# Q/K and first FFN contract in paired 64-row halves: seven steps of two halves that swap banks, in place of three full tiles and a 64-row rest

## The chip, the cores and the metric

The kernel runs on one core of one Trainium2 chip. The metric is the device time of one execution in microseconds (us); lower is better. TensorE is called PE, VectorE DVE, ScalarE ACT, GpSimd POOL and the DMA-issuing SyncE SP, as in the profile; PEld is PE's weight load.

## The reference

One adaLN transformer block with a sliding local dilated attention and a SiLU FFN, in bf16, batch 1, 2048 tokens, model width 448, 16 heads of 28, FFN width 1792:

```python
mod = (_silu(c) @ w_mod).reshape(c.shape[0], 6, 1, -1)
sa, ca, ga, sb, cb, gb = (mod[:, i] for i in range(6))   # shifts, scales, gates
h = _layernorm(x) * (1 + ca) + sa
x = x + ga * attention(h, wqkv, wo)      # 8 keys: positions s, s-2, ..., s-14
h = _layernorm(x) * (1 + cb) + sb
x = x + gb * (_silu(h @ w1) @ w2)
```

Each token attends to eight keys of its own parity (dilation 2, window 8). The contract dimension of Q, K, V, of the output projection and of the first FFN product is 448, which is three and a half times the 128 rows of PE's array; that of the second FFN product is 1792, fourteen times 128.

## The kernel before, in words

Tokens come in four chunks of 512 (NC = 4); within a chunk, even and odd positions are kept apart (`par`, 256 each). Every chunk goes through layer norm 1, the projections to Q, K and V, the attention in blocks of 112 or 128 queries (nine blocks by two parities), the output projection, layer norm 2, and two FFN products.

**The contract of 448.** Normalised activations are transposed so that the 448 features lie on partitions in four tiles that start at features 0, 128, 192 and 320 (`ROW`), so that tiles 1 and 2 overlap by 64. `tile_of(k, way)` gives for a "way" 0 or 1 three full tiles (0, 1 + way, 3) and as a fourth the 64 rows that are left: way 0 finds them in the upper 64 partitions of tile 2, way 1 in the lower 64 of tile 1. Two products, one of each way, thus have three 128-row matmuls each and one 64-row matmul in opposite halves of the array. These two run side by side. Weights for the rest rows are kept apart (`wp3` for Q and K, `w13` for the FFN).

**`duo`** (L556) writes this for Q and K (L619, 128 weights by 512 tokens, group pairs g, g+1) and for the first FFN product (L790, hidden tiles i and i + 7). A "member" of a duo is one double PSUM bank `[128, 2, 512]`, in which bank j holds the way-j product. A pair of members has two steps on PE, which may be separated by other work: `first` runs the six full matmuls of member 0, its two rest halves, and the two rest halves of member 1; `second` runs the six full matmuls of member 1. Member 0 is read out after `first`, member 1 after `second`. There are 8 pairs of Q/K, 12 pairs in the first FFN product, and 4 lone members there (i = 6) that have six full matmuls and two halves.

**PSUM.** Three double banks (`big`) serve V, Q/K, the logits (two at a time), the output projection and the first FFN product; two single banks (`one`) serve the attention's values and the second FFN product. A double bank is reused only when its reader is done: ACT or DVE casts (`qk<-ps_qk`, L623), ACT's exponentials (`p<-ps_l`, L679), ACT's SiLU (`both<-ps_h`, L794; it writes the tile named `both`, the hidden activations).

**Row modes.** PE works on 128 rows (most matmuls), on 64 (the rest halves of L619, L643, L763 and L790) or on 28 rows of a quarter (the logits, L671). V and the output projection place their rest halves first or last, by the parity of the block.

**The order.** The program is built as a list of operations with dependencies; `ORDER` is a list written out by hand that fixes the order in which they are issued, and by it the order on each engine. Each engine takes its instructions in that order. SP issues all DMAs, among them the transposes of normalised activations (`h<-xn`) and of attention outputs (`oT<-o`). The change leaves `ORDER` and the number of operations as they are.

A second copy of the whole layer (`safe`) stands behind a branch that is taken when a softmax sum is out of range; it isn't run here.

Of the kernel before, what the change touches and what calls it, by code (L numbers as in the profile page):

```python
# [16 lines left out]
H = 16  # L17
# [15 lines left out]
CP = 256  # L33
# [41 lines left out]
def half(j):  # L75
    return slice(K3 * j, K3 * j + K3)
# [8 lines left out]
def tile_of(k, way):  # L85

    return (slice(0, 128), (0, 1 + way, 3)[k]) if k < 3 else (half(1 - way), 2 - way)
# [129 lines left out]
def layer(ctx, tc, io, safe):  # L217
# [5 lines left out]
    V, S, G, T = nc.vector, nc.scalar, nc.gpsimd, nc.tensor  # L223
# [10 lines left out]
    def ct(shape, name, dt=BF16):  # L234
        return const.tile(shape, dt, name=name)

    def bigt(name):
        return big.tile([128, 2, 512], F32, name=name, tag="big")
# [17 lines left out]
    wp = ct([128, 3, 2 * H, 32], "wp")  # L256
    wp3 = ct([128, H, 32], "wp3")
# [3 lines left out]
    w1 = ct([128, 3, F], "w1")  # L261
    w13 = ct([128, F // 2], "w13")
# [41 lines left out]
    def none(o):  # L304
        pass

    P = Plan()
    for r, n in (("big", 3), ("one", 2), ("v", NV), ("p", NP), ("xn", NX), ("o0", 2), ("o1", 2), ("out", len(outb))):
        P.resource(r, n)

    def copy_on(o):
        return S.copy if o["eng"] == "act" else V.tensor_copy

    def either(act, dve):
        return [("act", act), ("dve", dve)]

    def act_ns(n):
        return 55.0 + 0.833 * n

    def dve_ns(n):  # L320
        return 75.0 + 1.04 * n

    P.resource("dma", 8)
    begin = P.op(("sp", 1630.0), none)

    def sp(ns, fn, deps, land=0.0, give=()):

        a = P.op(("sp", ns), fn, deps, take=("dma",))  # L330
        return P.op(("none", land), none, [a], give=((a, "dma"),) + tuple(give)), a

# [5 lines left out]
    def first_x(i):  # L338
        return dict(out=x_all[:, 2 * i:2 * i + 2, :].rearrange("p t d -> p (t d)"), in_=x_view[0, :, i, :])
    act_q = [P.op(("none", 0.0), lambda o: nc.scalar.dma_start(**first_x(1)))]  # L340
    act_q.append(P.op(("none", 0.0), lambda o: nc.scalar.dma_start(out=c4[0:3, :], in_=c[:, 0:384].rearrange("o (k p) -> (o k) p", p=128)), act_q[-1:]))
# [214 lines left out]
    def duo(mms, name, n, deps, evacs, table=None):  # L556


        held = {}
        ns = n / 2.4 + 2.0  # L560

        def first(o):
            p0 = held[0] = bigt(name)
            for j in range(2):
                for k in range(3):
                    mms[0](p0, j, k, k == 0, False)
            if len(mms) > 1:
                held[1] = bigt(name)
            for j in range(2):
                mms[0](p0, j, 3, False, True)  # L570
            if len(mms) > 1:
                for j in range(2):
                    mms[1](held[1], j, 3, True, False)

        def second(o):
            for j in range(2):
                for k in range(3):
                    mms[1](held[1], j, k, False, k == 2)
        mm = [P.op(("pe", 6 * ns + 110.0 + len(mms) * (ns + 12.0)), first, deps, take=("big",) * len(mms), mac=(6 + len(mms)) * ns, mode=(0, 1))]
        if len(mms) > 1:  # L580
            mm.append(P.op(("pe", 6 * ns + 5.0), second, [mm[0]], mac=6 * ns))
        out_ = []
        for i, ev in enumerate(evacs):
            last = [P.op(on, lambda o, f=f, i=i: f(o, held[i]), [mm[i]] + d, table=table) for on, f, d in ev]
            P.op(("none", 0.0), none, last, give=((mm[0], "big"),))
            out_.append(last)
        return mm, out_
# [23 lines left out]
    def project(k):  # L611
        h = h1[k % NH]
        s0 = CP * k

        def mm(g):
            def f(ps, j, kk, start, stop):
                rows, t = tile_of(kk, j)
                w = wp[:, kk, H * j + 4 * g:H * j + 4 * g + 4, :] if kk < 3 else wp3[rows, 4 * g:4 * g + 4, :]
                T.matmul(ps[:, j, :], lhsT=w.rearrange("p h d -> p (h d)"), rhs=h[rows, :, t, 128:128 + CP], start=start, stop=stop)  # L619
            return f  # L620

        def ev(g):
            return [(either(act_ns(1024), dve_ns(1024)), lambda o, ps: copy_on(o)(out=qk[:, :, g, :, s0:s0 + CP], in_=ps[:].rearrange("p j (t s) -> p j t s", t=2)), [])]  # L623
        qk_done[k], qk_mm[k], v_mm[k] = [], [], []
        for g in (0, 2):
            m, ev_ = duo([mm(g), mm(g + 1)], "ps_qk", 512, h1_done[k] + pads, [ev(g), ev(g + 1)])
            qk_mm[k] += m
            qk_done[k] += ev_[0] + ev_[1]

        def vev(o, ps, b):  # L630
            v_of[b] = vb[o["slot"]["v"]]
            copy_on(o)(out=v_of[b][:, :, :, 0:DH], in_=ps[:, :, 0:D].rearrange("p j (h d) -> p j h d", d=DH))
        for b in BLOCKS[k]:
            held = {}

            def vmm(o, b=b, held=held):
                ps = held[0] = bigt("ps_v")
                b0 = 128 + 112 * b - CP * k
                ks = (0, 1, 2, 3) if b % 2 == 0 else (3, 0, 1, 2)
                for kk in ks:  # L640
                    for par in range(2):
                        rows, t = tile_of(kk, par)
                        T.matmul(ps[:, par, 0:D], lhsT=h[rows, par, t, b0:b0 + 128], rhs=wv[rows, t, :], start=(kk == ks[0]), stop=(kk == ks[-1]))  # L643
            a = P.op(("pe", 1440.0), vmm, h1_done[k] + ([halo[k]] if k else []) + ld_v, take=("big",), mac=1309.0, mode=(b % 2, 1 - b % 2))
            v_mm[k].append(a)
            v_op[b] = a
            v_take[b] = P.op(either(act_ns(2 * D), dve_ns(2 * D)), lambda o, b=b, held=held: vev(o, held[0], b), [a] + v_ready, take=("v",), give=((a, "big"),))
# [129 lines left out]
    def us_of(k):  # L777
        return [4 * k + j for j in range(4)]

    def ffn1(k, after, l_before):  # L780
        h = h2[k % 2]
        nrm = Norm(us_of(k), x1_done, after=f1_read.get(k - 2, []), how=HOW2[k], scratch=screp[:].rearrange("p k n -> p (k n)")[:, 0:D])
        nrm.on_dma(lambda j: h[:, j:j + 2, :, :].rearrange("p j k t -> p (j k) t"), lambda t: h[:, :, t, :], 2, [mod2])

        def mm(i):
            def f(ps, j, kk, start, stop):
                rows, t = tile_of(kk, j)
                c0 = 128 * (i + 7 * j)
                w = w1[:, kk, c0:c0 + 128] if kk < 3 else w13[rows, 128 * i:128 * i + 128]
                T.matmul(ps[:, j, :], lhsT=w, rhs=h[rows, :, t, :], start=start, stop=stop)  # L790
            return f

        def ev(i):
            return [(("act", act_ns(1024)), lambda o, ps: S.activation(out=hid[:, k % 2, :, i, :], in_=ps[:], func=ACTF.Silu), after + f2_read.get(k - 2, []) + wmod_read)]  # L794
        f1_read[k], silus[k] = [], []
        for i in (0, 2, 4, 6):
            ii = [i, i + 1] if i < 6 else [i]
            mm_, ev_ = duo([mm(x) for x in ii], "ps_h", 512, nrm.done + ld_1 + l_before, [ev(x) for x in ii], table="s")
            f1_read[k] += mm_
            for e in ev_:  # L800
                silus[k] += e
# [93 lines left out]
@with_exitstack  # L895
def kernel(
    ctx: ExitStack,
    tc: tile.TileContext,
    A_x: bass.AP,
    A_wqkv: bass.AP,  # L900
    A_wo: bass.AP,
    B_x: bass.AP,
    B_w1: bass.AP,
    B_w2: bass.AP,
    c: bass.AP,
    w_mod: bass.AP,
    out: bass.AP,
):
    io = (A_x, A_wqkv, A_wo, B_w1, B_w2, c, w_mod, out)
    with ExitStack() as first:  # L910
        with tc.manual_schedule():
            bad = layer(first, tc, io, False)
    with tc.If(bad > 0, label="safe"):
        with ExitStack() as again:
            layer(again, tc, io, True)
# [30 lines left out]
```

## Time and profile before

| | us |
|---|---|
| median of 3 runs | 182.13 (181.04 to 182.39) |
| the profiled execution | 181.66 |
| its span, first to last instruction | 179.6 |
| mean granted TensorE clock | 0.994 of full speed |
| L790 (first FFN product), PE busy | 47.3, 224 matmuls |
| L812 (second FFN product), PE busy | 46.1, 224 matmuls |
| L619 (Q and K), PE busy | 26.8, 128 matmuls (20.0 and 6.8 in two groups, by the names of their tiles) |
| L794 (SiLU on ACT), busy | 28.0, 28 activations |

A row of the page's list of groups gives line, engine, operation, what is written from what, shapes and count; then busy time, the mean of one in ns, and the idle time of the engine just before such an instruction with what ended it. Matmuls are pipelined: a matmul of 512 columns is shown with 380 ns, but the next one starts 216 ns after it, so that the starts, not the durations, tell what a step costs. The chain that ended last is given as start, length, engine, tile, line and count; on a busy PE, a length there is the distance between the first starts of two groups.

### The profile page before, as it was taken

How to read it: one execution, taken by the hardware profiler on the slowest of the kernel's cores; microseconds unless marked ns; L12 is line 12 of the kernel's file. 1: busy time of each engine (PE TensorE's matmuls, PEld its weight loads, DVE VectorE, ACT ScalarE, POOL GpSimd, SP SyncE). 2: the span in 40 equal slices, each digit the busy share in tenths (PEclk: the TensorE clock that was granted, in tenths of full speed). 3: DMA queues.
4: the chain of work that ended last, by engine and by line, in shares of the span. 5: the costliest groups of instructions: out<-in, count | busy, mean ns of one | idle time of the engine just before them, and what ended most of it. 6: DMA issues, size and time to landing. Idle time of an engine off the chain costs nothing.

```text
span 179.6 us, 3554 instructions
## 1 busy us (share of the span) xinstructions
PE 168.7 (94%) x1406; PEld 76.7 (43%) x1406; DVE 103.9 (58%) x219; ACT 110.1 (61%) x153; POOL 26.1 (15%) x86
## 2 busy tenths in 40 slices
PE   7999999888889999999999999999999998999990
PEld 2543333444345344344544445554434444434540
DVE  5699797699798988364378135984633311200211
ACT  2277939897779657779999649643596322244200
POOL 4656540000012220022000000023040000000000
PEclk9999999999999999999999999999999999999997
DMA  5993569956682223102400013125307000010021
GB/s 199 333 344 89 143 143 305 336 117 152 185 251 55 51 62 84 26 0 62 58 26 4 26 26 80 29 55 135 84 0 194 5 0 26 0 51 4 29 79 35
DMA packets 33343, 17.42 MB, mean 97 GB/s; under 512 B 24296, under 2 KB 32936, under 8 KB 33320
## 3 DMA queue, kind: packets, MB, share of 16 engines
q1 hardware_dynamic: 33168, 16.90, 35.0%
q8 instruction: 13, 0.21, 0.5%
q10 hardware_dynamic: 152, 0.23, 0.4%
q14 instruction: 10, 0.08, 0.2%
HBM read 9.12 MB, written 1.84 MB: 61 GB/s over the span
## 4 chain that ended last, share of the span: by engine, by line
PE 70%; DVE 10%; DMA 7%; ACT 6%; POOL 3%; issue 2%; SPq 0%; ACTq 0%; DVEq 0%
PE ps_h L790 25%; PE ps_y L812 24%; PE ps_wo L763 7%; PE ps_qk L619 5%; PE ps_v L643 4%; ACT p L679 2%; PE ps_o L729 2%; DMA oT<-o 2%; DMA x_all<-in_A_x_dram 2%; DVE p L703 2%; DVE st L455 2%; PE ps_l L671 2%; ACT xn L483 2%; DMA wqk<-xn 2%; DMA h<-xn 2%
## 5 line engine op out<-in xcount | busy, mean ns | idle before, releaser
L790 PE MATMUL ps_h<-h,w 128*128 128x512 bf16 (+1 forms) x224 | 47.3, 380 | 0.0
L812 PE MATMUL ps_y<-w,both 128*128 128x448 bf16 x224 | 46.1, 353 | 0.6 <-DVE flag L884 0.6
L794 ACT ACTIVATE both<-ps_h 128x1024 bf16<-128x1024 f32 x28 | 28.0, 1022 | 26.0 <-PE ps_h L790 25.9
L679 ACT ACTIVATE p<-ps_l 128x896 bf16<-128x896 f32 (+1 forms) x36 | 30.7, 933 | 2.2 <-PE ps_l L671 2.1
L812 PEld LDWEIGHTS <-both 128*128 128x128 bf16 x224 | 20.8, 98 | 20.6 <-issue 1.6
L790 PEld LDWEIGHTS <-w 128*128 128x128 bf16 (+1 forms) x224 | 16.9, 96 | 27.0 <-issue 11.4
L817 DVE TENSOR_TENSOR ot<-ps_y,x_all 128x448 bf16<-128x448 f32 x16 | 9.8, 621 | 30.2 <-PE ps_y L812 30.1
L619 PE MATMUL ps_qk<-h,wp 128*128 128x512 bf16 (+1 forms) x96 | 20.0, 380 | 0.4 <-DVE h L542 0.4
L703 DVE TENSOR_TENSOR p<-p,maskb 128x1792 bf16<-128x1792 bf16 (+1 forms) x18 | 19.5, 1098 | 0.5 <-ACT p L679 0.5
L465 ACT ACTIVATE screp<-x_all,mv 128x448 bf16<-128x448 bf16 x16 | 10.7, 666 | 9.9 <-POOL mv L462 9.5
L619 PEld LDWEIGHTS <-wp 128*128 128x128 bf16 (+1 forms) x128 | 9.3, 97 | 16.1 <-issue 6.1
L462 POOL TENSOR_SCALAR mv<-sums 128x2 f32<-128x2 f32 x10 | 3.4, 343 | 76.0 <-DVE x_all L766 75.9
L766 DVE SCALAR_TENSOR_TENSOR x_all<-ps_wo,x_all 128x448 bf16<-128x448 f32 x16 | 9.5, 620 | 7.7 <-PE ps_wo L763 7.7
L485 DVE TENSOR_SCALAR xn<-x_all,mv,rs 128x512 bf16<-128x512 bf16 x23 | 8.8, 406 | 8.6 <-POOL rs L472 8.4
L763 PE MATMUL ps_wo<-wo,oT 128*128 128x448 bf16 (+1 forms) x64 | 12.5, 354 | 1.0 <-DMA oT<-o 0.6
L643 PE MATMUL ps_v<-wv,h 128*128 128x448 bf16 (+1 forms) x56 | 11.1, 354 | 1.0 <-ACT p L679 0.7
L623 DVE CAST qk<-ps_qk 128x1024 bf16<-128x1024 f32 x10 | 12.0, 1214 | 0.1
L472 POOL TENSOR_TENSOR rs<-rs,negh 128x2 f32<-128x2 f32 x16 | 11.5, 717 | 1.3
L735 DVE TENSOR_TENSOR o<-ps_o,rc 112x448 bf16<-112x448 f32 (+1 forms) x18 | 11.2, 624 | 0.6
L729 PE MATMUL ps_o<-v,p 128*128 128x29 bf16 x288 | 9.6, 176 | 1.2 <-DVE gbc L438 0.6
L542 DVE TENSOR_SCALAR h<-h,modc 128x512 bf16<-128x512 bf16 x15 | 5.6, 407 | 8.6 <-DMA h<-xn 8.6
L729 PEld LDWEIGHTS <-p 128*128 128x128 bf16 x288 | 8.8, 96 | 4.1 <-DVE p L703 0.9
(85 smaller groups left out, 147.9 us busy)
## 6 DMA issues: line engine op xcount, KB each, us to landing
out_dram<-ot SPq DMA_DIRECT2D x16, 112.0 KB, 1.7
both<-in_w_mod_dram SPq DMA_DIRECT2D x2, 672.0 KB, 5.7
x_all<-in_A_x_dram SPq DMA_DIRECT2D x3, 448.0 KB, 5.8
w<-in_B_w_dram SPq DMA_DIRECT2D x3, 448.0 KB, 6.0
w<-in_B_w_dram SPq DMA_DIRECT2D x1, 896.0 KB, 5.0
both<-in_w_mod_dram SPq DMA_DIRECT2D x2, 336.0 KB, 3.4
w<-in_B_w_dram SPq DMA_DIRECT2D x1, 672.0 KB, 5.2
wv<-in_A_wqkv_dram SPq DMA_DIRECT2D x2, 224.0 KB, 5.0
```

Source lines behind the costliest of these rows:

```text
L472: G.tensor_tensor(out=rs[:, j:j + n], in0=rs[:, j:j + n], in1=negh[:, 0:n], op=ALU.pow)
L619: T.matmul(ps[:, j, :], lhsT=w.rearrange("p h d -> p (h d)"), rhs=h[rows, :, t, 128:128 + CP], start=start, stop=stop)
L623: return [(either(act_ns(1024), dve_ns(1024)), lambda o, ps: copy_on(o)(out=qk[:, :, g, :, s0:s0 + CP], in_=ps[:].rearrange("p j (t s) -> ...
L643: T.matmul(ps[:, par, 0:D], lhsT=h[rows, par, t, b0:b0 + 128], rhs=wv[rows, t, :], start=(kk == ks[0]), stop=(kk == ks[-1]))
L679: S.activation(out=out_, in_=ps[:, :, 0:4 * nq].rearrange("p j (g q) -> p j g q", q=nq), func=ACTF.Exp, scale=SCALE)
L703: V.tensor_tensor(out=p, in0=p, in1=maskb[:, 1 if b == 0 else 0, 0:nq].unsqueeze(1).to_broadcast([128, H, nq]), op=ALU.mult)
L729: T.matmul(ps[:, h, 0:DH + 1], lhsT=p[:, at:at + 128], rhs=v[:, h, 0:DH + 1], start=True, stop=True)
L735: V.tensor_tensor(out=box["o"][0:nq, off:off + D].rearrange("p (h d) -> p h d", d=DH), in0=ps[0:nq, :, 0:DH], in1=r.unsqueeze(2).to_broadc ...
L763: T.matmul(ps[:, par, 0:D], lhsT=oT[rows, kk, par, s0:s0 + 128], rhs=wo[rows, par, kk, :], start=(q == qs[0]), stop=(q == qs[-1]))
L790: T.matmul(ps[:, j, :], lhsT=w, rhs=h[rows, :, t, :], start=start, stop=stop)
L794: return [(("act", act_ns(1024)), lambda o, ps: S.activation(out=hid[:, k % 2, :, i, :], in_=ps[:], func=ACTF.Silu), after + f2_read.get(k ...
L812: T.matmul(box["ps"][:, 0:D], lhsT=hid[:, k % 2, f % 2, f // 2, 128 * j:128 * j + 128], rhs=w2[:, f // 2 + 7 * (f % 2), :], start=(f == 0) ...
```

## The change

Only `duo` and the two functions that give it its matmuls (`mm` in `project` and in `ffn1`) change, and only for pairs in the main copy; the lone members and the `safe` copy keep the old order.

Every matmul of a pair now has 64 rows. A full 128-row tile is issued as two matmuls, `part` 0 on partitions 0 to 63 and `part` 1 on 64 to 127. In the **straight** part of a member, four steps, the lower half goes to bank 1 and the upper half to bank 0 (the rest rows kk = 3 lie that way by themselves: bank j uses half 1 - j). In the **crossed** part, three steps, the lower half goes to bank 0 and the upper to bank 1. Two matmuls of one step thus lie in opposite halves of the array and write different banks. After a straight part comes a drain marked fusable that increments a semaphore `turn`; a crossed part starts with a wait for that count.

For a pair, `first` now issues straight(0), straight(1) and crossed(0): eleven steps; `second` issues crossed(1): three. Before it was eight and six. Both members' banks are taken in `first` as before, member 1's from the fifth step on.

```diff
+    turns = []
+    if not safe:
+        turn = tc.alloc_semaphore("turn")
...
     def duo(mms, name, n, deps, evacs, table=None):
...
+        def passed(i):
+            T.drain(fusable=True).then_inc(turn, 1)
+            turns.append(i)
+            wait[i] = len(turns)
+
+        def straight(i):
+            held[i] = bigt(name)
+            for kk in (0, 3, 1, 2):
+                for part in range(2):
+                    mms[i](held[i], 1 - part, kk, kk == 0, False, part)
+            passed(i)
+
+        def crossed(i):
+            T.wait_ge(turn, wait[i])
+            for kk in range(3):
+                for part in range(2):
+                    mms[i](held[i], part, kk, False, kk == 2, part)
+
         def first(o):
+            if len(mms) > 1 and not safe:
+                straight(0)
+                straight(1)
+                crossed(0)
+                return
             p0 = held[0] = bigt(name)
...
         def second(o):
+            if not safe:
+                return crossed(1)
             for j in range(2):
...
         def mm(i):
-            def f(ps, j, kk, start, stop):
+            def f(ps, j, kk, start, stop, part=None):
                 rows, t = tile_of(kk, j)
+                rows = half(part) if kk < 3 and part is not None else rows
                 c0 = 128 * (i + 7 * j)
-                w = w1[:, kk, c0:c0 + 128] if kk < 3 else w13[rows, 128 * i:128 * i + 128]
-                T.matmul(ps[:, j, :], lhsT=w, rhs=h[rows, :, t, :], start=start, stop=stop)
+                w = w1[rows, kk, c0:c0 + 128] if kk < 3 else w13[rows, 128 * i:128 * i + 128]
+                return T.matmul(ps[:, j, :], lhsT=w, rhs=h[rows, :, t, :], start=start, stop=stop)
             return f
```

`mm` of `project` changes in the same way with `wp` and `wp3`.

More of the change, by code (lines that the diff above doesn't have):

```diff
@@ L556, in duo @@
     def duo(mms, name, n, deps, evacs, table=None):
-        held = {}
+        held, wait = {}, {}
         ns = n / 2.4 + 2.0
-        def first(o):
+        def passed(i):
[13 more added lines that the diff above has]
+                    mms[i](held[i], part, kk, False, kk == 2, part)
+        def first(o):
+            if len(mms) > 1 and not safe:
[3 more added lines that the diff above has]
+                return
             p0 = held[0] = bigt(name)
@@ L615, in mm @@
         def mm(g):
-            def f(ps, j, kk, start, stop):
+            def f(ps, j, kk, start, stop, part=None):
                 rows, t = tile_of(kk, j)
-                w = wp[:, kk, H * j + 4 * g:H * j + 4 * g + 4, :] if kk < 3 else wp3[rows, 4 * g:4 * g + 4, :]
-                T.matmul(ps[:, j, :], lhsT=w.rearrange("p h d -> p (h d)"), rhs=h[rows, :, t, 128:128 + CP], start=start, stop=stop)
+                rows = half(part) if kk < 3 and part is not None else rows
+                w = wp[rows, kk, H * j + 4 * g:H * j + 4 * g + 4, :] if kk < 3 else wp3[rows, 4 * g:4 * g + 4, :]
+                return T.matmul(ps[:, j, :], lhsT=w.rearrange("p h d -> p (h d)"), rhs=h[rows, :, t, 128:128 + CP], start=start, stop=stop)
             return f
@@ L785, in mm, with f @@
         def mm(i):
-            def f(ps, j, kk, start, stop):
+            def f(ps, j, kk, start, stop, part=None):
                 rows, t = tile_of(kk, j)
+                rows = half(part) if kk < 3 and part is not None else rows
                 c0 = 128 * (i + 7 * j)
-                w = w1[:, kk, c0:c0 + 128] if kk < 3 else w13[rows, 128 * i:128 * i + 128]
-                T.matmul(ps[:, j, :], lhsT=w, rhs=h[rows, :, t, :], start=start, stop=stop)
+                w = w1[rows, kk, c0:c0 + 128] if kk < 3 else w13[rows, 128 * i:128 * i + 128]
+                return T.matmul(ps[:, j, :], lhsT=w, rhs=h[rows, :, t, :], start=start, stop=stop)
             return f
```

## The prediction

> **What bounds the kernel now.** I read the page's busy shares and its chain first:
>
> ```profile
> PE 168.7 (94%) x1406; PEld 76.7 (43%) x1406; DVE 103.9 (58%) x219; ACT 110.1 (61%) x153; POOL 26.1 (15%) x86
> PE 70%; DVE 10%; DMA 7%; ACT 6%; POOL 3%; issue 2%; SPq 0%; ACTq 0%; DVEq 0%
> ```
>
> PE (TensorE) is 70% of the chain. Where is it the bound? The table of stretches (length, then busy time by engine) says from 58.8 us on:
>
> ```profile
> 46.40:58.80 12.40, 11.24 (x168) 6.07 (x169) 10.66 (x20) 10.27 (x16) 1.62 (x4) 1.00 0.62 168
> 58.80:94.80 36.00, 35.91 (x295) 15.64 (x295) 22.89 (x44) 27.90 (x40) 4.75 (x12) 1.00 0.22 46
> 94.80:129.40 34.60, 34.60 (x326) 16.76 (x323) 21.44 (x48) 21.54 (x30) 3.04 (x10) 1.00 0.23 57
> 129.40:175.00 45.60, 44.95 (x229) 19.55 (x227) 9.46 (x22) 17.99 (x23) 2.17 (x6) 1.00 0.13 38
> ```
>
> After 58.8 PE is idle for 0.74 us in 116; what it saves or loses there is the kernel's. Before, DMA, ACT (ScalarE) and DVE (VectorE) end most waits. What a matmul step costs is in the chain in order of time (start, us, what, count):
>
> ```profile
> 77.06 6.47 PE ps_h L790 x32
> ...
> 102.66 1.30 PE ps_h L790 x6
> ...
> 104.36 3.24 PE ps_h L790 x16
> ```
>
> Six full matmuls (a pair's second half alone) take 1.30: **0.217 us a step**. A whole pair (x16) is 12 full matmuls and 2 steps in which two 64-row halves run side by side: 14 steps, 3.03, and 0.21 is left. Two pairs in a row (x32) are 28 steps, 6.07, and leave 0.40. In the starts of single matmuls the rest sits at the two changes of row mode: the step into 64 rows is 0.311, the one back 0.309, and the first after each is longer by 0.006 to 0.010. So **a change of mode costs 0.10 us**, and a pair has two.
>
> **The arithmetic of the change.** Per tile of a pair it replaces 3 full steps per bank (6) and one shared rest step by 7 steps of two halves: 7 steps either way. Twenty pairs (8 of Q/K, 12 of the first FFN contract; its four lone tiles stay) have 280 steps before and after. Matmuls go from 16 to 28 a pair, 240 more in all, and as many weight loads.
>
> *Price of a half step when many follow each other.* The trace has at most three in a row, where Q/K meets V, both in 64-row mode:
>
> ```profile
> 60.42 2.00 PE L619 MATMUL ps_qk<-h,wp 128*128 128x512 bf16 x10
> 62.25 1.59 PE L643 MATMUL ps_v<-wv,h 64*128 64x448 bf16 x8
> ```
>
> From 60.42 to 62.25 are 8 steps (1.73) and one change (0.10): nothing is left over, so two half steps and the crossing into the next group's half step cost what full ones do. The logits (L671) put four 28-row matmuls side by side for four rounds and, at 51.45 in the PE timeline, take 0.31 with their exit: 4 x 0.047 (112 columns at the full rate) and 0.10, although 8 instructions go into each 0.05 us; a half step has 4 in 0.217. Bounds: 0.213 (the crossing step just shown) and 0.226 (a first step after a change, were every step like it). I take 0.217. Over the 196 steps of the 14 pairs after 58.8 the bounds are -0.7 and +1.8 us.
>
> *The weight loads.* Of their groups, L790's has 96 ns a load; in full steps one starts 2 ns after the running matmul and ends inside its step. The trace shows two 64-row loads starting 3 ns apart under two running halves (78.30). So they are hidden at 0; were that cover gone, a step would grow by 0.096.
>
> The Trainium skill ("TensorE: Matmul & The Clock Gate", The mechanism, in Part 3) says that weight loads overlap running matmuls only where their row groups differ. The full steps, where load and matmul share all rows, contradict it; by it the price would be the last one.
>
> *Changes of mode.* I walked PE's groups in order of time and counted where the row mode changes: **104 before, 91 after**. A pair between full-row work has two either way. Pairs next to each other, or next to V, the projection or a lone tile that ends in halves, lose some (from 15.3, 25.5, 48.1, 76.9, 131.2 us). A second part that full-row work separates from its first has none now and gets two (102.5, 150.2, 163.6). Before 46.4 us 8 of 29 go, from 46.4 to 58.8 3 of 14, after that 2 of 61: 77 to 94 loses two, 129 to 148 two, 148 to 175 gains two. Worth after 58.8: 2 x 0.10 = **-0.20**.
>
> *The drains.* Two a pair, 40. They are marked fusable: the increment may ride on the matmul before them, and nothing else signals from that matmul (the results are read only after the crossed steps). Matmuls that signal today keep their 0.216 step. I take 0. If a drain stands in PE's stream and waits until the array is empty, the next load starts only then: ACT sees a tile's end 0.43 after the start of its last matmul (78.29 to 78.72), plus 0.05 for a semaphore instruction on PE's sequencer, less the step of 0.217: 0.27 each. That is the upper end.
>
> The Trainium skill ("PSUM — Partial Sum Buffer", Engine vs sequencer instructions) says that a drain waits for the engine to go fully idle; no mid-stream drain is in this trace. By it the second rival would come about.
>
> *The added waits* (`turn`). Behind them queue the crossed steps and all later PE work. The first crossed part waits for a straight part that ended four steps (0.87) earlier; the second, if it follows at once, for one whose last matmul started 0.87 earlier and signals after 0.43: 0.44 in hand, half a step's loads need 0.1. Cost 0; with nothing in hand 0.1 a pair.
>
> *What comes later.* The first tile's last step moves from the pair's 7th to its 11th: +0.57 (no change at entry, and an earlier start) to +0.87 us. Its reader and the PSUM bank it frees (three double banks) move with it. The second tile also takes its bank at step 5 instead of 8. I followed each bank and reader through the trace:
>
> - Before 46 us: readers slip by up to 0.9, but the wait on the output transposes at 46.57 (0.57 long) and the exponentials' table load at 30.2 end last. 0.
> - 46 to 59, a chain of ACT and PE:
>
> ```profile
> 49.95 1.01 ACT L623 CAST qk<-ps_qk 128x1024 bf16<-128x1024 f32 x1 [1.51 <-PE ps_qk L619]
> 51.32 0.67 ACT L465 ACTIVATE screp<-x_all,mv 128x448 bf16<-128x448 bf16 x1 [0.36 <-POOL mv L462]
> 51.98 3.32 ACT L679 ACTIVATE p<-ps_l 128x896 bf16<-128x896 f32 x4
> ...
> 53.74 1.61 PE L643 MATMUL ps_v<-wv,wqk 64*128 64x448 bf16 x8 [0.43 <-ACT p L679]
> ...
> 58.89 0.74 PE L763 MATMUL ps_wo<-wo,oT 64*128 64x448 bf16 x3 [0.44 <-ACT p L679]
> ```
>
> The pair at 48.11 starts at 48.01 (its entry change is gone), its first tile's last step at 48.01 + 10 x 0.217 = 50.18, and ACT's cast at 50.60 instead of 49.95. It ends at 51.61; L465 behind it starts there instead of at 51.32, and the exponentials, back to back with it, move by **+0.29**. PE waits for just these at 53.74 and 58.89 (last two rows), so all after them moves by 0.29. PE's three saved changes are lost in those waits.
> - 77 to 115: the pairs at 76.9 give 0.20. From 109.97 six exponentials run back to back on ACT, and two of the logits groups there start 0.04 and 0.12 after the bank they need came free. The activation before them waits behind a tile that is 0.87 later, so ACT is not earlier; I let the 0.20 be eaten: +0.20.
> - After 115: each silu that slips is read at least 0.9 us later, or runs after its pair's second tile (143.2, 152.6). 0.
>
> **Sum** on the profiled execution (181.66 us, span 179.6, so 2.06 around it): -0.20 + 0.29 + 0.20 = **+0.3, 181.95**. The median of the runs, 182.13, is 0.47 above that execution: **182.4**. A measurement of this kernel tells about 1% (1.8 us) from nothing.
>
> **Rivals.**
>
> - *Nothing is late, the saved changes stay.* The 0.29 and 0.20 vanish and the five changes from 46.4 on count: 181.6; with the eight before them too 180.8, and with half steps at the lower bound 180.1. Against it: ACT ends the waits at 53.74 and 58.89. Chance 0.08, half of it for the last two.
> - *The drains stand* (the slower side): after 58.8 28 x 0.27 = 7.6 us, and up to 12 x 0.27 = 3.2 before: **190 to 193**. It decides as soon as the increment cannot ride on the last straight matmul. For it: PE has drains today only at its start and end; against it: the marking, and one signal per matmul leaves room. Chance 0.10.
> - *Long half steps*: every one costs 0.226, so 182.4 + 1.8 = **184.2**, to 184.8 with a late `turn` here and there. For it: the only half steps next to a change are that long. Against it: the third step at 62.25. Chance 0.10.
> - *Weight loads uncovered* in half mode: 196 x 0.096 = 18.8: **201**. Against it: the loads at 78.30. Chance 0.03.
> - *It doesn't do what it says*: the halves run one after the other because they share a bank. The straight part sends them to two banks, and the signal orders the swap; I count this into the last case.
>
> **Numbers.** Forecast 182.4, chance 0.69, own range 181.6 to 183.4 (both terms of the lateness gone or doubled). 80%: **181.0 to 184.8**, which leaves out the standing drains (0.10), the uncovered loads (0.03) and half of the first rival (0.04). Faster by over 1% (under 180.3) 0.04, that half; slower by over 1% (above 183.95) 0.10 + 0.03 + 0.08 of the long steps + 0.02 = 0.23; within 1% 0.73.
>
> **What will show it.** PE 1646 matmuls; L790 in a pair alone still 3.2 us on the chain, two pairs at 77 us 6.27 instead of 6.47; no drain inside PE's stream; the weight loads' waits on issue fewer by about 13 in all; ACT's cast near 50.6; the wait at 53.74 longer. Half steps of 0.222 and more, drains with a gap of 0.27 behind them, or loads outside the matmuls would prove me wrong; so would waits of PE on silu results (L794), which I put at none.

## The result, and the profile after

The changed kernel takes **183.06 us** (median of 20 runs, 182.32 to 185.0), the kernel before 182.06 (20 runs): a ratio of **1.007, interval 1.0046 to 1.0093**. The forecast was 182.4 with 181.0 to 184.8: the sign and the range held, but the loss is 1.0 us, not 0.3, and the traces show that it comes from something that no term of the prediction named. That sign and range held all the same is luck.

The half steps themselves do what was expected. (Lines move down in the changed kernel: Q/K L619 is L651, the first FFN product L790 is L823, the cast L623 is L655, the output projection L763 is L795, the logits L671 are L703.) Chain in order of time of the changed kernel (start, us, what, count), from 104 to 109 us and from 66 to 78 us:

```profile
104.16 0.75 PE ps_h L823 x6
...
105.41 3.13 PE ps_h L823 x28
```

```profile
66.35 4.48 DMA h<-xn
70.83 0.02 issue
70.85 0.02 ACTq L544
70.86 0.05 issue
70.91 0.82 ACT h L544
71.73 0.04 issue
71.78 5.13 PE ps_h L823 x36
76.90 1.43 PE ps_wo L795 x8
```

A pair alone (x28) takes 3.13 us, 14 steps of 0.216 and one mode change, where before it was 3.24. (That is no gain: its other change of mode now falls at the end of the group ahead of it, which takes 0.50 instead of 0.39.) No drain stands in TensorE's (PE's) stream, and 1645 of the 1646 matmuls are recorded. But ahead of the first FFN contract stands a row that the chain of before does not have: the second transpose of normalised activations takes 4.48 us, and PE waits for it. The chain of before in the same place has PE alone, one group behind the other:

```profile
70.20 0.50 PE ps_o L729 x16
70.70 4.93 PE ps_h L790 x24
75.63 1.43 PE ps_wo L763 x8
```

The waits of PE (what waited, for what: us in total, times, longest), of before and then of after:

```profile
PE ps_wo L763 <- DMA oT<-o: 0.6, 1, 0.6
```

```profile
PE ps_h L823 <- ACT h L544: 1.4, 1, 1.4
...
PE ps_l L703 <- DVE qk L655: 0.7, 2, 0.5
PE ps_l L703 <- ACT qk L655: 0.6, 2, 0.3
```

One wait on a DMA has gone, and a larger one has come: PE waits for ACT's h, and ACT for the late transpose. By the starts of PE's groups in the two traces, the 1.27 us between the spans (179.55 and 180.82) are made of:

| stretch | before | after | difference |
|---|---|---|---|
| start to the output projection near 46 us | 46.57 | 46.05 | -0.52 |
| from there to the next one, near 59 us | 12.32 | 12.52 | +0.20 |
| from there to the first FFN contract | 11.66 | 13.21 | **+1.55** |
| from there to the last matmul | 104.04 | 104.01 | -0.03 |
| last matmul to the end | 4.96 | 5.03 | +0.07 |

**What delays the transpose?** The page's DMA queues name a queue that carries code:

```profile
q8 instruction: 13, 0.21, 0.5%
```

```profile
q8 instruction: 15, 0.25, 0.6%
```

The first is before, the second after (packets, MB, share of the DMA engines' time). The packets are of 16 KB and take about 1 us; between two of them PE executes some 250 instructions (matmuls and weight loads; 194 to 291 between 35 and 138 us in the two traces), so this is taken to be PE's program, loaded in blocks as PE goes along. The count of packets, and their shifts when PE's warm-up is edited below, agree with that. The change adds 240 matmuls and 240 weight loads, two blocks, and moves all the others. Before, a block came at 64.08, into the *first* transpose of that pair (4.25 us, and nothing on PE waited for it), and another at 44.5, into an oT<-o transpose that the projection at 46.57 waited for (issued at 42.65, 3.88 us). After, a block comes at 68.44, 2.09 us behind the issue of the *second* h<-xn, and none is near 44.

The Trainium skill ("Runtime: NRT & Kernel Launch", Instruction fetch mechanics) says that an engine's code is refilled in 16 KiB blocks of 256 instructions and that this is mostly hidden. The traces agree on the block (245,760 bytes in 15 packets). PE is not seen waiting for its code; what the experiments below test is whether a transpose is.

### The profile page after: what moved, and what is told of

The parts are those of the page before. It is cut to its first block, busy times and chain, and to the rows that moved or that the text cites. A ratio compares the mean times of both kernels' runs of the same rounds, so it can differ in the third digit from the quotient of the medians.

```text
span 180.8 us, 4033 instructions
## 1 busy us (share of the span) xinstructions
PE 167.9 (93%) x1645; PEld 79.3 (44%) x1646; DVE 104.1 (58%) x219; ACT 109.5 (61%) x153; POOL 25.9 (14%) x86
## 4 chain that ended last, share of the span: by engine, by line
PE 69%; DVE 9%; ACT 7%; DMA 4%; POOL 4%; issue 3%; ACTq 0%
PE ps_h L823 25%; PE ps_y L845 24%; PE ps_qk L651 7%; PE ps_wo L795 5%; PE ps_v L675 4%; DMA h<-xn 2%; PE ps_o L761 2%; ACT qk L655 2%; POOL rs L476 2%; PE ps_l L703 2%; DVE st L459 2%; DMA x_all<-in_A_x_dram 2%; ACT p L711 1%; ACT screp L469 1%; DVE p L735 1%
## 5 line engine op out<-in xcount | busy, mean ns | idle before, releaser
L823 PE MATMUL ps_h<-h,w 64*128 64x512 bf16 (+1 forms) x368 | 45.4, 377 | 1.4 <-ACT h L544 1.4
L827 ACT ACTIVATE both<-ps_h 128x1024 bf16<-128x1024 f32 x28 | 27.3, 1021 | 26.8 <-PE ps_h L823 26.7
L845 PEld LDWEIGHTS <-both 128*128 128x128 bf16 x224 | 20.3, 98 | 21.7 <-issue 4.2
L823 PEld LDWEIGHTS <-w 64*128 64x128 bf16 (+1 forms) x368 | 18.0, 94 | 26.3 <-issue 6.9
L651 PE MATMUL ps_qk<-h,wp 64*128 64x512 bf16 x168 | 19.4, 377 | 0.5 <-ACT qk L655 0.4
L651 PEld LDWEIGHTS <-wp 64*128 64x128 bf16 x224 | 11.1, 94 | 13.7 <-issue 1.5
L795 PE MATMUL ps_wo<-wo,oT 128*128 128x448 bf16 (+1 forms) x64 | 12.5, 354 | 0.4 <-ACT p L711 0.4
L655 DVE CAST qk<-ps_qk 128x1024 bf16<-128x1024 f32 x10 | 12.1, 1219 | 1.1 <-PE ps_qk L651 1.0
```

Source lines behind the costliest of these rows:

```text
L651: return T.matmul(ps[:, j, :], lhsT=w.rearrange("p h d -> p (h d)"), rhs=h[rows, :, t, 128:128 + CP], start=start, stop=stop)
L795: T.matmul(ps[:, par, 0:D], lhsT=oT[rows, kk, par, s0:s0 + 128], rhs=wo[rows, par, kk, :], start=(q == qs[0]), stop=(q == qs[-1]))
L823: return T.matmul(ps[:, j, :], lhsT=w, rhs=h[rows, :, t, :], start=start, stop=stop)
L845: T.matmul(box["ps"][:, 0:D], lhsT=hid[:, k % 2, f % 2, f // 2, 128 * j:128 * j + 128], rhs=w2[:, f // 2 + 7 * (f % 2), :], start=(f == 0) ...
```

## Experiments

**Theory 1**: a block of PE's code that is loaded while a DMA transpose is under way delays that transpose; the change moved a block into the transpose that the first FFN contract waits for, and that is the loss. **Theory 2**: the half steps, or the later end of each pair's first tile, make h late in some other way. To move the blocks without touching the work, the warm-up is edited: 27 matmuls of 512 columns at the start, whose results nobody reads. Leaving some out, or cutting some in narrower pieces, shifts every later instruction of PE against the block borders.

### The same edit in both kernels: fewer fillers

```diff
-junks = [P.op(("pe", 428.0), lambda o: warm_up(2), [w_last], mac=426.0) for _ in range(JUNK)]
+junks = [P.op(("pe", 428.0), lambda o, i=i: warm_up(2 if i < 2 else 0), [w_last], mac=426.0) for i in range(JUNK)]
```

(`i < 6` in b_j6.) The changed kernel, a_j2:

> The changed kernel with 16 of its 20 filler matmuls on TensorE left out (they only warm the engine; nothing reads them). TensorE's instructions come 32 earlier in its stream, so by the instruction positions of the changed kernel's trace the block of TensorE's code that was loaded at 68.4 us is loaded near 70.0, behind the second h<-xn transpose. Theory 1 (a code load inside a transpose's window delays its landing): that transpose takes 2.7 to 2.9 us instead of 4.48, TensorE's wait on h of 1.4 us in the first FFN contract goes, and the time is 181.5 to 182.3 us (the upper end if the block that moves from 39.4 to near 41.3 delays an oT<-o transpose there). Theory 2 (the transpose is late for another reason that the change brings, its half steps or the order of its tiles): 4.3 to 4.6 again, 182.8 to 183.4 us.

The kernel before, b_j2 and b_j6:

> The kernel before with the same 16 filler matmuls left out. Its code block of 64.1 us then comes near 67.3, into the second h<-xn transpose, and the one of 44.5 near 48.1, out of the oT<-o transposes that TensorE waits for at 46.57. Theory 1: the second h<-xn takes 4.2 to 4.6 us instead of 2.72, TensorE waits 1.2 to 1.4 us for it, and the wait of 0.57 at 46.57 goes: 182.8 to 183.5 us, the loss that the change showed, with no half step in the program. Theory 2: 2.7 to 2.9 us and 181.8 to 182.4 us.

> The kernel before with 8 of the 20 filler matmuls left out. The blocks of 44.5 and 64.1 us come near 46.6 and 65.8, outside the transposes that TensorE waits for. Theory 1: the wait of 0.57 at 46.57 goes and nothing is lost at 70: 181.4 to 182.1 us; beside the changed kernel with its blocks out of the way this shows what the change itself is worth. Theory 2: 181.8 to 182.4 us, no transpose faster.

Measured: a_j2 182.75 (181.5 to 184.75), b_j2 182.85 (ratio to before 1.0051, 1.0031 to 1.007), b_j6 181.81 (0.9992, 0.997 to 1.0013). In a_j2 the block came at 73.6 and the second h<-xn took 2.73: theory 1 holds for the transpose, though its time is above the range. The profile has two other losses: the projection near 46 us starts 1.0 us later than in the changed kernel, and PE's granted clock is 0.88 from 46 to 60 us, which makes that stretch 1.7 us longer (next group of runs). Whether the missing fillers bring these on was not tested. In b_j2 and b_j6 the aim was missed: the blocks did not move as reckoned (65.7 and 64.1 instead of 67.3 and 65.8; 44.2 and 44.3 instead of 48.1 and 46.6), so neither decides between the theories at the place they were made for. A block seems to be called for ahead of the instructions that run, and by how far varies; that is argued, not shown. In b_j2 the wait before the projection at 46 is 1.19 us, not gone as expected, with a block at 44.21 in the oT<-o issued at 42.90; and its next chunk's h<-xn takes 3.81, with a block 0.54 us behind its issue.

### The changed kernel with its blocks moved

```diff
-    warm = []
+    warm, cuts = [], []
...
-            T.matmul(warm[0][:, 0, :], lhsT=junk[:, 0:128], rhs=junk, start=True, stop=True)
+            cuts.append(1)
+            for c in ((0, 256, 512) if len(cuts) <= 24 else (0, 512),):
+                for a, b in zip(c, c[1:]):
+                    T.matmul(warm[0][:, 0, a:b], lhsT=junk[:, 0:128], rhs=junk[:, a:b], start=True, stop=True)
```

> The changed kernel with 24 of the 27 warm-up and filler matmuls cut into two of half the width: the same busy time, 48 more TensorE instructions before the work. The code block of 68.4 us then comes near 65.6, between the two h<-xn transposes, and the one of 49.1 near 46.1, behind the oT<-o transposes that TensorE waits for. Theory 1: the second h<-xn takes 2.7 to 2.9 us, no wait of TensorE on h, 181.3 to 182.0 us. Theory 2: 4.3 to 4.6 us as before, 182.8 to 183.4 us.

Measured: **181.36** (180.89 to 183.67), 1.7 us under the changed kernel, and against before a ratio of 0.9987 (0.9959 to 1.0015). The block came at 65.2 and the second h<-xn landed in 2.72. The chain there is PE's again, with no row of DMA between 60 and 80 us:

```profile
69.92 0.50 PE ps_o L764 x16
70.42 4.85 PE ps_h L826 x36
75.27 1.43 PE ps_wo L798 x8
```

A control is `len(cuts) <= 8`, the same edit with 16 instructions instead of 48:

> The changed kernel with 8 of its warm-up matmuls cut in two, 16 instructions more instead of the 48 of the run that took 181.36 us. The block of 68.4 us then comes at 66.5 to 68, still behind the issue of the second h<-xn transpose. Theory 1: that transpose takes 3.2 to 4.7 us and the time stays at 182.5 to 183.4 us, although the warm-up was edited in the same way. Theory 2 (any edit of the warm-up cures the late transpose): 2.7 us and 181.3 to 181.8 us.

Measured: 182.62 (181.85 to 184.79); block at 68.72, 0.85 us behind the issue; the transpose took 3.83 and PE waited 0.8 us for it. Editing the warm-up is no cure by itself: what counts is where the block falls. The third run puts the same 48 instructions in another place (the last 8 fillers in four pieces each):

> The changed kernel with its last 8 filler matmuls cut into four of a quarter width: the same 48 more instructions as in the run that took 181.36 us, in another place and with the first warm-up left as it was. Theory 1: the block of 68.4 us comes between 64.5 and 66.3, the second h<-xn transpose lands in 2.7 us, 181.2 to 181.9 us. Theory 2: 4.5 us and 182.8 to 183.4 us.

Measured: 182.5 (181.21 to 185.93), above the range, although the transpose took 2.73 us and PE did not wait (block at 67.0, ahead of the issue at 68.14). But for one (185.93) its runs lie in two heaps: six of 181.21 to 182.25 us, with a mean granted clock of 0.996 to 1.0, and five of 182.74 to 183.07, with 0.987 to 0.991. The profile is of the upper heap and shows why; busy time by stretch (length, PE, PEld, DVE, ACT, POOL, granted clock, DMA share, GB/s), a_late48 and then a_p48:

```profile
46.00:60.00 14.00, 12.99 (x182) 6.71 (x181) 11.08 (x21) 10.58 (x16) 1.31 (x4) 0.88 0.68 150
```

```profile
46.00:60.00 14.00, 12.82 (x190) 6.93 (x188) 12.59 (x24) 12.15 (x18) 1.62 (x4) 1.00 0.55 148
```

Between 46 and 60 us the granted clock is 0.88, and the way from one output projection to the next takes 14.19 us instead of 12.52. The profiles of a_j2 and a_p16 have the same dip (0.88 over that stretch); in that of the changed kernel the clock there is 1.00. So a_late48's upper heap is the dip's, not a transpose's; the median of its lower heap, 181.5, lies in the range of theory 1. (a_p48 has three such runs, 182.71 to 183.67 at 0.984 to 0.989. In a_p16 only the profiled run and the longest have so low a clock, so its 182.62 is not the dip's. a_j2's runs lie in two heaps too, but there the shorter ones have the lower mean clock, 0.978 to 0.981, so that the dip alone does not part them.) What brings the dip on was not tested.

### The mirror: blocks moved in the kernel before

Here the first 23, 7 or 13 warm-up matmuls are cut into five pieces and the others into four, which gives 208, 176 or 188 instructions more:

```diff
-    warm = []
+    warm, cuts = [], []
...
-            T.matmul(warm[0][:, 0, :], lhsT=junk[:, 0:128], rhs=junk, start=True, stop=True)
+            k, m = len(cuts), (5, 23, 4)
+            cuts.append(1)
+            m = m[0] if k < m[1] else m[2]
+            c = [512 * i // m for i in range(m + 1)]
+            for a, b in zip(c, c[1:]):
+                T.matmul(warm[0][:, 0, a:b], lhsT=junk[:, 0:128], rhs=junk[:, a:b], start=True, stop=True)
```

> The kernel before with its 27 warm-up and filler matmuls cut into four or five narrower ones: 104 more matmuls, 208 more TensorE instructions ahead of the work, no half step. By instruction positions the code block of 85.1 us then comes near 68.9, into the second h<-xn transpose, and the one of 44.5 near 40 and 50, out of the oT<-o transposes that TensorE waits for at 46.57. The blocks of the last runs came up to 2.6 us away from such a reckoning, so what counts is where the trace shows it. Theory 1, with the block between 66.4 and 69.1: that transpose takes 4.2 to 4.6 us, TensorE waits 1.2 to 1.5 us in the first FFN contract, 182.5 to 183.4 us (up to 0.5 more if the narrower matmuls lengthen the start); with the block outside: 2.7 us, no wait. Theory 2: 2.7 us wherever the block is.

Measured: **183.88** (ratio 1.0091, 1.0063 to 1.0119). The block came at 65.4, in front of the second h<-xn, which took 2.72, as theory 1 says of a miss. The next block, however, came at 86.34, 1.24 us behind the issue of the *next chunk's* h<-xn, which took 4.67 us (3.33 in the kernel before). The chain of this run:

```profile
85.10 4.67 DMA h<-xn
89.77 0.02 issue
89.79 0.02 ACTq L545
89.81 0.05 issue
89.86 0.81 ACT h L545
90.67 1.62 ACT p L684 x2
92.29 0.04 issue
92.33 0.37 PE ps_l L676 x14
```

The exponentials are queued on ACT behind the late modulation, and PE's logits wait 0.95 us for them, in two waits; before, the chain between 84 and 97 us is PE's alone. From the first FFN contract to the last matmul it is 105.28 us instead of 104.04: +1.24, with no half step in the program. That is a loss like the change's, made in the kernel before at another transpose. (Of its span's 2.27 us more, 0.45 are lost ahead of the first FFN contract and 0.58 behind the last matmul.)

> The kernel before with 88 more warm-up matmuls (the same width in narrower pieces), 176 TensorE instructions more, no half step. The last three shifts left the code block that comes between 61 and 70 us at almost the same place (64.1 to 65.4), in front of the second h<-xn transpose; this one should put it at 66.5 to 70. Theory 1, if the trace shows it 0.1 to 2.2 us behind the issue of that transpose: it lands in 3.2 to 4.7 us instead of 2.72, TensorE waits up to 1.4 us at the first FFN contract, and that contract starts up to 1.4 us later against the transpose's issue than in the run with 104 more matmuls. Theory 2: 2.7 us. If the block misses the window again, the run says nothing of it.

> The kernel before with 94 more, narrower warm-up matmuls, 188 TensorE instructions more, no half step. With 176 more the code block came at 70.9 us, behind the second h<-xn transpose, with 208 more at 65.4, in front of it; 188 should put it between. Theory 1, if the trace shows it 0.1 to 2.2 us behind the transpose's issue: landing in 3.2 to 4.7 us instead of 2.72, and the first FFN contract starts 4.7 to 5.5 us after that issue instead of 3.87, as in the changed kernel. Theory 2: 2.7 and 3.9 us.

Measured: 182.48 (1.0015, 0.9986 to 1.0043) and 182.3 (1.0001, 0.9977 to 1.0025). The blocks came at 70.9 and 69.4, both behind the landing; the transposes took 2.73 and the contract started 3.88 us after the issue. So the mirror at this very transpose was not brought about. These two are useful otherwise. In b_p176 a block at 57.72 comes 2.08 us behind the issue of an oT<-o, which takes 4.27 us, and PE waits for it in the projection near 59 us:

```profile
60.05 1.59 PE L768 MATMUL ps_wo<-wo,oT 64*128 64x448 bf16 x7 [0.68 <-DMA oT<-o]
```

From that projection to the first FFN contract it is 12.59 us instead of 11.66, again with no half step in the program. In b_p188 no transpose that PE waits for is hit by a block (the wait at 46.57 is gone too), which makes it the partner for a_p48.

### All transposes together

The time that a transpose takes is counted from its issue to its landing. From 55 us on, in the fourteen traces, all 62 h<-xn take 2.71 to 2.79 us for which no code block starts in the 1.6 us ahead of the issue or before the landing. Of such oT<-o, 92 take 2.28 to 2.38; five more were issued while a delayed transpose was still under way, and take up to 3.64. Ahead of 55 us, where the weights are loaded, transposes take longer without a block too. With a block of PE's queue, by when it starts behind the issue (h<-xn):

| block starts behind the issue by | the h<-xn takes | in |
|---|---|---|
| -1.00, -0.23, -0.17 (ahead) | 2.82, 2.71, 3.42 | f_only, a_stand, b_p176 |
| 0.10, 0.13, 0.16 | 2.88, 3.13, 3.20 | a_j2, q_only, a_j2 |
| 0.26, 0.46, 0.54 | 3.52, 3.33, 3.81 | b_j6, before, b_j2 |
| 0.85, 1.24 | 3.83, 4.67 | a_p16, b_p208 |
| 1.81, 2.09, 2.18 | 4.48, **4.48**, 4.25 | f_only, **after**, before |
| 2.34, 2.35, 2.57 | 2.75, 2.74, 2.72 | f_only, b_j6, a_stand |

The 2.82 and the 3.42 of the first row were issued while a delayed transpose was under way. The delay grows, not quite evenly, from nothing to between 1.5 and 1.9 us with the time that the transpose has been under way, and there is none with a block from 2.34 us on. The oT<-o do much the same: 3.0 to 4.0 with the block at 0.6 to 1.1 us, 3.8 to 4.4 at 1.2 to 2.1, 2.28 to 2.37 from 2.32 on. It is the same in both kernels. The wait at 46 us fits too: in the five profiles with a block 1.3 to 1.9 us behind the issue of the second oT<-o there (before, b_j2, b_j6, b_p208, f_only) PE waits 0.57 to 1.19 us for it, in the nine others not at all. Theory 1 is shown, for the transposes and, by a_p48, a_p16, b_p208 and b_p176, for the wait of PE behind them; theory 2 has nothing left to explain.

### Each part alone

> Only the first FFN contract in half steps, Q/K as before the change, nothing else. Up to 70 us TensorE's instructions are those of the kernel before, so its code blocks are too. Theory 1: the second h<-xn transpose takes 2.7 us, TensorE does not wait for it, the wait of 0.57 at 46.57 stays: 181.6 to 182.2 us. Theory 2 (the FFN's half steps or the order of their tiles make the loss of 1 us): 182.8 to 183.4 us.

> Only the Q/K pairs in half steps, the first FFN contract as before the change, with 24 warm-up matmuls cut in two as in the run that was already made with the whole change (181.36 us). Theory 1 (the FFN's half steps by themselves are worth nothing, because the 0.20 us saved at 77 is eaten behind 110): 181.2 to 181.7 us. Rival (the saved changes of mode in the FFN stay): 181.6 to 182.0 us.

(Against the changed kernel; q_only has the warm-up of a_p48 besides.)

```diff
+        halves = name == "ps_h"           # "ps_qk" in q_only
-            if len(mms) > 1 and not safe:
+            if len(mms) > 1 and halves and not safe:
...
-            if not safe:
+            if halves and not safe:
```

Measured: f_only 182.2 (1.0, 0.998 to 1.0021), q_only 182.17 (1.0016, 0.9988 to 1.0044). f_only is as theory 1 has it: second h<-xn 2.73, no wait for it, and 0.61 for the oT<-o at 46.39. q_only's median lies above the ranges of both readings. Four of its twelve runs, 183.06 to 183.79 us, have a mean clock of 0.987 to 0.989; the other eight, 181.56 to 182.5, have a median of 181.9, which would be the rival's, but this is sorted after the fact. Its profile, of 182.5 us, has 5.72 us behind the last matmul instead of 4.96.

The traces decide its question better. A start has to be taken that half steps don't shift, so the projection near 59 us and not the first FFN contract, whose change of mode on entry now falls ahead of its first matmul. From there to the output projection that starts a little after 115 us it is 56.85 us in before, 56.94 in b_j6, 56.86 in b_p188 and 56.96 in q_only, but **56.70** in f_only, 56.69 in a_p48 and 56.70 in a_late48. So 0.16 us of the FFN's saving is kept, against theory 1's reading, but not all of it: up to the group `ps_o` at 107 us f_only and a_p48 are ahead by 0.33 and 0.34. In between stand the three groups of logits (before, and then a_p48):

```profile
107.99 0.31 PE ps_l L671 x16
...
111.07 0.31 PE ps_l L671 x16
...
112.62 0.31 PE ps_l L671 x16
```

```profile
107.40 0.34 PE ps_l L706 x16
...
110.52 0.37 PE ps_l L706 x16
...
112.12 0.38 PE ps_l L706 x16
```

Before, the last two groups start 0.12 and 0.04 us behind the end of the exponentials that free a bank for them; in a_p48 one matmul in each waits until 0.05 us behind that end. These groups are held up by 0.16 us in all.

In the profile of after nothing is left of the saving from the first FFN contract on (45.17 us to the projection near 117, 45.19 before, 44.96 in a_p48). It is lost at the start: the first group of that contract, up to the next projection, takes 4.96 us instead of 4.75, since its fourth step starts at 72.48, just behind ACT's second half of h (72.43); from there to the later projection it is 40.21 us in both. In a_p16, where h is late too, it is 4.97 and 45.17.

### What a standing drain costs

```diff
-            T.drain(fusable=True).then_inc(turn, 1)
+            T.drain(fusable=False).then_inc(turn, 1)
```

with the warm-up cut as in a_p16, but 16 of them.

> The changed kernel with its 40 drains marked as not fusable, and 16 of the 27 warm-up matmuls cut in two (32 instructions more, so that TensorE's code blocks again stay out of the transposes that it waits for). This prices the rival of the prediction. If a drain that stands waits until the array is empty: 0.27 us each, 28 of them after 58.8 us and up to 12 before, 189 to 192.5 us beside 181.4 of the changed kernel with its blocks moved, and a gap of about 0.27 behind each straight part. If it is only one more instruction on the sequencer: 181.3 to 182.3 us and no gaps.

Measured: **190.99** (ratio 1.0486, 1.046 to 1.0511). Two pairs in a row, from their first matmul to the next group, in stretches of PE (length, busy, clock, DMA share, GB/s), a_stand and then a_p48:

```profile
80.18:87.37 7.19, 6.86 (x58) 1.00 0.17 39
```

```profile
76.63:82.78 6.15, 6.15 (x57) 1.00 0.18 42
```

Four drains cost 1.04 us, **0.26 each**. From the projection near 59 us to the last matmul it is 122.80 instead of 115.55: 7.25 us for 28 drains, 0.26 again. The rule of the Trainium skill that the prediction set beside this rival ("PSUM — Partial Sum Buffer", Engine vs sequencer instructions: a drain waits for the engine to go idle) agrees with the standing drain here, at 0.26 us each; the fusable one costs nothing that the trace shows.

## Why the prediction was right in sign and too small

**The failing step is in the arithmetic of the change: "Matmuls go from 16 to 28 a pair, 240 more in all, and as many weight loads."** It priced the 480 instructions by PE's time only (steps, weight loads, mode changes). They are also two more blocks of code (15 for 13), and all later blocks moved; against the transposes that was worth -0.5 us at 46 and +1.5 at 70 us, more than all the terms that were reckoned. The trace of before held the warning: 13 packets in the instruction queue, one of them in the oT<-o that PE waited 0.57 us for, and one in an h<-xn that took 4.25 us beside its neighbour's 2.72. Which transposes the moved blocks would hit could not have been reckoned from it, as the runs that missed their aim show; a place in the range could have been given. The prediction also took "the wait on the output transposes at 46.57 (0.57 long)" as fixed; where no block lies in those transposes (after, a_p48, b_p188) it is gone.

*By its own terms.* For the term from 46 to 59 us, the chain of after has the cast and the logits that wait for it:

```profile
50.08 1.02 ACT qk L655
51.10 0.04 issue
51.14 0.40 PE ps_l L703 x14
```

- **Half steps 0.217, weight loads 0: right.** A pair alone is 3.13, two pairs at 78 us 6.15 (6.27 was forecast, 6.47 it was; of the 0.32 less, 0.10 now falls into the group ahead). That makes 28 steps of 0.216 and one change of mode. The waits of weight loads on issue fell from 100 to 84, by 16 where 13 were forecast; on the two changed lines by 22. 28 steps in 6.15 us leave no time for the loads of 0.094 us each beside them, so the loads are hidden. The Trainium skill's sentence that was set against this ("TensorE: Matmul & The Clock Gate", The mechanism, in Part 3: loads overlap only where row groups differ) does not hold here; the same section also names loads into a background weight buffer, a case that the prediction left out and that these numbers would fit.
- **Drains 0, `turn` waits 0, no wait on silu: right**, and the rival's 0.27 for a standing drain measured 0.26; its 190 to 193 us would have been 191.
- **46 to 59 us, +0.29: the mechanism right, the size about 0.2.** ACT's cast was to start 2.59 us after its pair, and did so after 2.58 (47.50 to 50.08). PE's logits wait for this cast, and the exponentials start 5.60 us behind the projection (46.05 to 51.65) instead of 5.41 (46.57 to 51.98). From one projection to the next it is 12.51 or 12.52 us in after, a_p48 and q_only, which have the Q/K half steps and no dip, and 12.32 to 12.38 in six of the seven profiles without half steps in Q/K; the seventh, b_p176, has 12.55, with a wait of 0.93 us on a DVE cast. The wait at 53.74 did not grow (0.44 at 53.41).
- **-0.20 saved after 58.8, and +0.20 "eaten" from 109.97 on: the mechanism of both right, the saving mis-sized.** 0.34 us were saved by 107 us: mainly the two changes of mode at 77, as forecast, and in the group before them a wait of 0.07 us for the second half of h, which the prediction did not count. The logits ate 0.16 of it, 0.13 by the banks that the prediction named, and 0.16 stay (56.69 against 56.85). The profiled run of after lost even that behind the late h.
- **The change by itself**: with blocks out of the way in both, the last matmul starts at 174.17 us (a_p48) and 174.13 (b_p188), one profile of each. By these the half steps and the saved changes are worth nothing either way (about +0.2 at 46 to 59 us, -0.16 after), and the +0.3 of the sum was an overestimate by that much; the 1.0 us measured are the blocks'. The medians of the two, 181.36 and 182.3, differ mostly by the part behind the last matmul (4.95 and 5.67 in the profiles). The first rival ("nothing is late") is in part what the traces show after 59 us.

Not settled: what brings on the dip of the clock at 46 to 60 us, why the part behind the last matmul varies from 4.8 to 5.7 us, and by what a transpose is slowed while a block is loaded. The medians of a_p48 (181.36) and before (182.0) can't be told apart by their interval, and a_late48, with the same count of instructions, has 182.5; so no version here is shown to beat the kernel before.

## What to carry to other kernels

A change that adds instructions to an engine also moves the loading of its code: look up the instruction queue's packets in the trace of before, ask which later ones may fall into DMA transposes that something waits for (where they land could be reckoned here only to within some 4 us), and give that its own place in the range. Before an unexpected difference of 1 us is explained by the edit, shift the instruction stream by a few dozen harmless instructions in both versions and see whether it stays. An increment on a drain marked as fusable cost nothing here, while a drain that stood in PE's stream cost 0.26 us each time.

## What the runs showed of the hardware

- A 16 KB block of PE's code, about 1 us on the queue, delays a DMA transpose under way by up to about 2 us, the more the longer the transpose has run, and an oT<-o issued behind a delayed one is late too (2.7 becomes up to 4.7 us for h<-xn, 2.3 up to 4.4 for oT<-o).
- The blocks do not follow PE's instructions rigidly: in the kernel before, 16 and 32 instructions fewer left the block of 64.1 us within 1.7 us; 208 more (48 short of 256) had one at 65.4, and 176 more (80 short) at 70.9. They were placed by trial.
- In three profiles an edited warm-up went with a granted clock of 0.88 between 46 and 60 us, 1.7 us each; in others (a_p48, b_j6) it did not.
